# Thresholded attention with a two-layer block on one core: the value product and its scaling placed later in each period, and a score bank for one second-layer group

## The chip, the cores and the metric

The kernel runs on one core of one Trainium2 chip. The metric is the device time of one execution in microseconds (us); the time of a kernel is the median of several executions. A profiled execution has two numbers: its own time, and the span from the first to the last instruction in its trace, which is a little shorter.

## The reference

For 8 batches, 8 heads, 576 positions and a head width of 64, attention with a threshold is followed by two dense layers over 4608 tokens.

```python
scores = (1 / sqrt(64)) * q @ k^T
thresh = max(scores, axis=-1) - tau                    # tau = 0.02
scores = where(scores >= thresh, scores, -1e9)
attn = exp(scores - max(scores));  attn /= sum(attn) + 1e-9
x = (attn @ v), heads side by side                     # 4608 x 512
h = x @ w_in                                           # 512 -> 2048
out = maximum(0.01 * h, h) @ w_out                     # 2048 -> 512
```

## The kernel before

**Periods.** The work is cut into N = 72 periods, and the loop at L653 writes out the instructions of one period after another; no planner reorders them, so each engine works through its own queue in that order. A period has 128 query rows of one batch and four heads (two pairs `c`, two halves `h`), that is four score tiles of 128 x 576. Every second batch also has two "tail" periods for the last 64 rows of each head. Two neighbouring periods give the four heads pairs of 128 tokens, which make one group for the two dense layers.

**Lags.** In the iteration n of the loop three periods are at work: `st`, period n, gets its scores; `before`, period n-1, has its weights `w` turned by DMA transposes on SP's queue (`turn_w`, L391); `due`, period n-2, gets its value product (`pv`, L434, 20 matmuls; 40 for a tail) and is then scaled by the reciprocal sums `by` into `x` (`evacuate`, L453, or L445 for tails, one VectorE instruction).

**TensorE's order in a period before the change.** Scores (`sc`, L297), transposes of the next queries and keys (`tp`, L186), a spread of the reciprocals (L414), then two half periods. The first half has two calls of `layer2` (8 matmuls into `o`, L507), one unit of `layer1` (32 matmuls into `hp`, L474), and `pv(due)`; the second half has again two calls of `layer2` and one of `layer1`. A group has four units of `layer1` (u = 0 to 3) and eight calls of `layer2` (r = 0 to 7). The units stand in the list `l1q`, which `evacuate` fills at the end of a group; a half that finds the list empty has no `layer1`. Each `layer1` releases the second-layer calls of the unit before it into `l2q`. Since two periods give four units and take four, the lists never hold much.

**VectorE's order.** Four copies of the scores out of PSUM with the row minimum (`copy_min`, L338; a copy of turned keys or queries, L249, comes after the first), the reciprocals (L385), the thresholds `th` (L356), then `x` (L453), then three masks (`weights`, L378), which read `th` as their scalar. ScalarE does the exponentials `e` (L367), the fourth tile's weights (L372, L373), the activation `g` of the first layer (L477) and the copy `osb` of a finished `o` (L511), among copies.

**PSUM.** The scores have five banks of their own (`sc`). The tag "h" has two banks, taken in turn by the transposes, `hp`, `pv` and `hp`. The tag "o" has one bank, so the first second-layer call of a group waits for the `osb` copy of the group before. In the last two periods `pv` goes into score banks, and the last group's second layer too (`layer2_last`). After n = 71 there are no scores; what remains of the value products and layers runs out over six more iterations of the loop, the drain.

Of the kernel before, what the change touches and what calls it, by code (L numbers as in the profile page):

```python
# [9 lines left out]
FP32 = mybir.dt.float32  # L10
# [23 lines left out]
def kernel(  # L34
# [341 lines left out]
    def weights(st, n):  # L376
        c, h = t = TILES[n]
        st.last = nc.vector.scalar_tensor_tensor(out=w_of(st, t), in0=st.s[t][:, :], scalar=st.th[:, n : n + 1],  # L378
                                                 in1=st.e[t][:, :], op0=AX.is_le, op1=AX.mult,
                                                 accum_out=st.sum[:, c, h : h + 1])  # L380
# [41 lines left out]
    def pv(st):  # L422
        if st.n >= N - 2:

            st.pv = sc[:, ds(1024 * (N - st.n), 256)].rearrange("d (c q) -> d c q", c=2)
        else:
            st.pv = ps.tile([128, 2, 128], FP32, tag="h", bufs=2, name="pv")
        n = 64 if st.tail else 128
        for c, u in ((c, u) for c in range(2) for u in range(128 // n)):
            pair = 2 * c + u if st.tail else 2 * st.pp + c  # L430
            for i in range(5):
                for h in range(2):
                    blk = i if h == 0 else 9 - i
                    nc.tensor.matmul(out=st.pv[ds(64 * h, 64), c, ts(u, n)], lhsT=v16[st.b % 2][:, pair, blk, :],  # L434
                                     rhs=st.wt[:, c, blk - (blk > 4), ts(u, n)],
                                     start=(i == 0), stop=(i == 4), skip_group_check=True)
# [3 lines left out]
    def evacuate(st):  # L440
        if st.tail:
            if st.b % 2 == 0:
                xs["t"] = sb.tile([128, NP, 128], FP16, tag="xt", bufs=2, name="xt")
            x = xs["t"]
            nc.vector.tensor_tensor(out=x[:, :, ds(64 * (st.b % 2), 64)],  # L445
                                    in0=st.pv[:, :, :].rearrange("d c (u q) -> d (c u) q", u=2),
                                    in1=st.by[:, :, :].rearrange("d c (u q) -> d (c u) q", u=2), op=AX.mult)
            new = [Group(x[:, :, :], (st.b - 1, None))] if st.b % 2 == 1 else []
        else:
            if st.pp == 0:  # L450
                xs["m"] = sb.tile([128, NP, 128], FP16, tag="x", bufs=4, name="x")
            x = xs["m"]
            nc.vector.tensor_tensor(out=x[:, ds(2 * st.pp, 2), :], in0=st.pv[:, :, :], in1=st.by[:, :, :], op=AX.mult)  # L453
            new = [Group(x[:, :, :], (st.b, st.m))] if st.pp == 1 else []
        l1q.extend((g, u) for g in new for u in range(4))
# [43 lines left out]
    def layer2():  # L499
        g, r = l2q.pop(0)  # L500
        if g.where == (B - 1, 3):
            return layer2_last(g, r)
        if r == 0:
            g.o = ps.tile([128, 512], FP32, tag="o", bufs=1, name="o")
        for j in (2 * r, 2 * r + 1):
            for c in range(2):
                nc.tensor.matmul(out=g.o[ds(64 * c, 64), :], lhsT=g.g[:, j, ds(64 * c, 64)],  # L507
                                 rhs=w_out16[:, j, :], start=(j == 0), stop=(j == 15), skip_group_check=True)
        if r == 7:
            g.out = sb.tile([128, 512], FP32, tag="osb", bufs=3, name="osb")  # L510
            nc.scalar.activation(out=g.out[:, :], in_=g.o[:, :], func=AF.Copy, bias=0.0, scale=1.0)  # L511
            stores.append(g)
# [139 lines left out]
    n = 0  # L652
    while n < N + PV_LAG or l1q or pending or l2q or stores:  # L653
        st = periods[n] if n < N else None
        before = periods[n - 1] if 1 <= n <= N else None
        due = periods[n - PV_LAG] if PV_LAG <= n < N + PV_LAG else None
        here = before and before.n < 3
        rest = due and due.n < 3
        plain = 2 if n < 2 or n == 4 else 3
        keys, now32, late = turns_at.get(n, []), early32.get(n, []), late32.get(n)  # L660


        if n == 0:
            def between():
                copy_min(st, 0)
                copy_min(st, 1)
                take_low(k32[1])
                for x in now32:
                    turn32(x)
            scores(st, between)  # L670
            turn32(late)
        elif st:
            scores(st)
        if rest:
            o = ps.tile([128, 1024], FP16, tag="o", bufs=1, name="wp")
            turn_w_here(due, 12, 6, o[:, 0:768])
        bank = turn(keys) if keys else None
        for x in now32 if n else []:
            turn32(x)
        if here:  # L680
            before.wt = sb.tile([128, 2, 9, 128], FP16, tag="wT", bufs=4, name="wT")
            bank = ps.tile([128, 1024], FP16, tag="h", bufs=2, name="tp")
        if due:
            bank = spread(due, bank)
        if here:
            turn_w_here(before, 0, 6, bank[:, 0:768])
        for key in keys:
            take(key, 0, on_act)
        if due:
            take_spread(due, bank)  # L690
        for x in now32:
            take_high(x)
        if here:
            take_w(before, 0, 6, bank[:, 0:768], on_act)
        if st:
            def taken():
                for key in keys:
                    take(key, 1, on_dve)
                if rest:
                    take_w(due, 12, 6, o[:, 0:768], on_dve)  # L700
            copies(st, before, taken, now32)
            exp_plain(st, 0)
            if n == 0:
                exp_plain(st, 1)
                take_high(late)
                take_low(late)
        elif before:
            recip(before)
        work = [lambda key=key: split_pool(key) for key in split_at_.get(n, [])] + pool_at.get(n, [])
        for i, f in enumerate(work):  # L710
            mm = f()
            if i == 0 and before:
                behind_masks(mm, before)
        for key in keys:
            if key[1:] == ("t", "k"):
                widen_keys(key[0])
        if n >= 5:

            for f in small_at.get(n, []):
                f(small=nc.gpsimd)  # L720
        if n < 4:
            idle((4, 10, 8, 4)[n], spare("o"))
        if here:
            o = ps.tile([128, 1024], FP16, tag="o", bufs=1, name="wp")
            if n < 3:
                turn_w_here(before, 6, 6, o[:, 0:768])
        elif before:
            turn_w(before, 1 if st else 2)
        for f in loads_at.get(n, []) + (small_at.get(n, []) if n < 5 else []):
            f()  # L730
        while stores and (n >= N or n not in loads_at or len(stores) > 1):
            store()

        if due and n == 3:
            pv(due)
        if n == 3:
            turn32(late)
            turn_w_here(before, 6, 6, o[:, 0:768])
        for half in range(2):
            if half == 1 and n in (3, 4):  # L740
                exp_steep(st, plain)
            for _ in range(2):
                if l2q:
                    layer2()
            if l1q:
                layer1()
            elif n >= N:
                settle()
            if half == 0:
                if st:  # L750
                    for i in range(1, plain if n else 0):
                        exp_plain(st, i)
                        if n == 3 and i == 1:
                            take_high(late)
                if here:
                    take_w(before, 6, 6, o[:, 0:768], on_act)
                if late and n not in (0, 3):
                    turn32(late)
                    take_high(late)
                if due:  # L760
                    if n != 3:
                        pv(due)
                    evacuate(due)
            elif st and n != 3:
                for i in range(plain + (n == 4), 4):
                    exp_steep(st, i)
        if n == 4:
            take_low(late)
        for i in range(plain if st else 0):
            weights(st, i)  # L770
            if late and n != 4 and n and i == 0:
                take_low(late)
        n += 1
# [33 lines left out]
```

## Time and profile before

| | |
|---|---|
| median of 3 executions | 480.15 us (477.99, 481.57, 480.15) |
| the profiled execution's own time | 480.22 us |
| its span | 478.40 us |
| mean granted TensorE clock | 0.996 |
| TensorE matmuls, busy | 462.8 us, 97% of the span |
| VectorE, busy | 431.6 us, 90% |
| ScalarE, busy | 419.1 us, 88% |
| GpSimd, busy | 216.2 us, 45% |

The busy time of TensorE comes from matmuls whose ends are modelled and overlap, so the pace is better read from the starts of successive blocks in the timeline. In the text below n is the number of the period; scores of period 9 start at 72.69 us, those of period 34 at 226.95 us, those of period 71, the last, at 452.88 us.

### The profile page before, as it was taken

How to read it: one execution, taken by the hardware profiler on the slowest of the kernel's cores; microseconds unless marked ns; L12 is line 12 of the kernel's file. 1: busy time of each engine (PE TensorE's matmuls, PEld its weight loads, DVE VectorE, ACT ScalarE, POOL GpSimd, SP SyncE). 2: the span in 40 equal slices, each digit the busy share in tenths (PEclk: the TensorE clock that was granted, in tenths of full speed). 3: DMA queues.
4: the chain of work that ended last, by engine and by line, in shares of the span. 5: the costliest groups of instructions: out<-in, count | busy, mean ns of one | idle time of the engine just before them, and what ended most of it. 6: DMA issues, size and time to landing. Idle time of an engine off the chain costs nothing.

```text
span 478.4 us, 25135 instructions
## 1 busy us (share of the span) xinstructions
PE 462.8 (97%) x10806; PEld 377.2 (79%) x10806; DVE 431.6 (90%) x1307; ACT 419.1 (88%) x782; POOL 216.2 (45%) x355
## 2 busy tenths in 40 slices
PE   6889889999999999999999999999999999999997
PEld 4667768888888888888888888888888888877776
DVE  3999969999999999999999999999999999999950
ACT  4898968999999999999999998999999999988862
POOL 2645646554465474455465574545357474000000
PEclk9999989999999999999999999999999999999999
DMA  9999998698899968799889987779889996765561
GB/s 174 236 218 195 188 225 164 156 204 178 201 162 192 246 147 210 117 188 203 186 185 182 210 187 176 150 181 202 189 190 173 200 214 129 117 131 124 123 146 46
DMA packets 208767, 84.26 MB, mean 176 GB/s; under 512 B 177648, under 2 KB 203504, under 8 KB 208656
## 3 DMA queue, kind: packets, MB, share of 16 engines
q1 hardware_dynamic: 201616, 75.25, 79.6%
q0 software_dynamic: 5568, 6.95, 7.7%
q8 instruction: 84, 1.38, 1.2%
q10 hardware_dynamic: 1472, 0.46, 0.4%
q14 instruction: 27, 0.22, 0.2%
HBM read 36.70 MB, written 9.44 MB: 96 GB/s over the span
## 4 chain that ended last, share of the span: by engine, by line
PE 87%; DVE 5%; DMA 4%; ACT 2%; issue 1%; SPq 0%; DVEq 0%; ACTq 0%
PE hp L474 25%; PE o L507 24%; PE sc L297 22%; PE pv L434 8%; DMA wT<-w 3%; PE tp L414 3%; PE tp L186 3%; DVE s L338 3%; DMA raw<-in_k_dram 1%; DVE w L378 1%; PE sc L486 1%; ACT g L477 0%; ACT s L372 0%; SPq L86 0%; ACT e L367 0%
## 5 line engine op out<-in xcount | busy, mean ns | idle before, releaser
L338 DVE TENSOR_SCALAR_CACHE_REDUCE s<-sc 128x576 f32<-128x576 f32 x288 | 205.5, 753 | 18.0 <-PE sc L297 17.9
L474 PEld LDWEIGHTS <-win 128*64 128x64 f16 x4608 | 147.1, 110 | 28.8 <-issue 1.3
L378 DVE SCALAR_TENSOR_TENSOR w<-s,th,e 128x576 f16<-128x576 f32 x213 | 163.6, 815 | 0.2
L367 ACT ACTIVATE e<-s,mn 128x576 f16<-128x576 f32 x213 | 157.8, 778 | 0.0
L507 PE MATMUL o<-wout,g 128*64 128x512 f16 x1120 | 145.0, 380 | 0.6 <-ACT osb L511 0.6
L474 PE MATMUL hp<-x,win 128*64 128x128 f16 x4096 | 137.1, 220 | 0.6 <-DVE x L453 0.3
L477 ACT ACTIVATE g<-hp 128x512 f16<-128x512 f32 x144 | 86.1, 598 | 42.8 <-PE hp L474 42.8
L297 PE MATMUL sc<-kT,qT 64*128 64x384 f16 (+7 forms) x1920 | 120.5, 284 | 2.2 <-DVE s L338 1.3
L297 PEld LDWEIGHTS <-qT 64*128 64x128 f16 (+1 forms) x1920 | 90.7, 97 | 18.6 <-issue 2.2
L160 POOL TENSOR_SCALAR scaled<-raw 128x512 f32<-128x512 f32 x53 | 32.7, 616 | 142.3 <-DVE w L378 129.5
L507 PEld LDWEIGHTS <-g 128*64 128x64 f16 x1120 | 56.8, 110 | 28.5 <-issue 0.7
L171 POOL TENSOR_TENSOR half<-scaled,half 128x512 f16<-128x512 f32 (+1 forms) x68 | 71.7, 1054 | 5.8
L373 ACT ACTIVATE w<-s,minus_tau 128x576 f16<-128x576 f32 x75 | 58.2, 775 | 2.4
L372 ACT ACTIVATE s<-s,th 128x576 f32<-128x576 f32 x75 | 57.5, 767 | 0.7 <-DVE th L356 0.7
L434 PE MATMUL pv<-wT,v 128*64 128x128 f16 (+1 forms) x1560 | 51.6, 214 | 3.7 <-DMA wT<-w 2.7
L434 PEld LDWEIGHTS <-v 128*64 128x64 f16 x1600 | 45.7, 110 | 5.1 <-DMA wT<-w 2.7
L167 POOL CAST half<-scaled 128x512 f16<-128x512 f32 (+1 forms) x68 | 38.3, 563 | 4.4
L453 DVE TENSOR_TENSOR x<-pv,by 128x256 f16<-128x256 f32 x62 | 26.3, 423 | 4.3 <-PE pv L434 4.2
L420 ACT COPY by<-tp 128x256 f16<-128x256 f16 x71 | 26.4, 372 | 0.0
L186 PEld LDWEIGHTS <-half 64*128 64x128 f16 x968 | 24.3, 95 | 2.6 <-issue 1.7
L186 PE MATMUL tp<-ident,half 64*128 64x64 f16 x968 | 24.2, 190 | 0.4 <-issue 0.4
L113 POOL CAST v<-vraw 128x256 f16<-128x256 f32 x64 | 24.5, 417 | 0.0
(64 smaller groups left out, 338.5 us busy)
## 6 DMA issues: line engine op xcount, KB each, us to landing
vraw<-in_v_dram SPq DMA_DIRECT2D x16, 512.0 KB, 5.5
out_dram<-osb SPq DMA_DIRECT2D x31, 256.0 KB, 3.9
raw<-in_q_dram SPq DMA_DIRECT2D x13, 512.0 KB, 4.8
raw<-in_k_dram SPq DMA_DIRECT2D x13, 512.0 KB, 5.5
win<-in_moe_w_in_dram POOLq DMA_DIRECT2D x4, 512.0 KB, 10.6
wout<-in_moe_w_out_dram POOLq DMA_DIRECT2D x4, 512.0 KB, 12.4
raw<-in_q_dram SPq DMA_DIRECT2D x12, 128.0 KB, 3.8
raw<-in_k_dram SPq DMA_DIRECT2D x10, 128.0 KB, 4.4
```

Source lines behind the costliest of these rows:

```text
L171: nc.gpsimd.tensor_tensor(out=halves[key][:, 1, 0:n, :, :], in0=scaled.pop(key)[:, 0:n, :, :], in1=halves[key][:, 0, 0:n, :, :], op=AX.sub ...
L186: nc.tensor.transpose(tps[key][r][:, x, t, :], half[rows, x, t, :, :].rearrange("p h d -> p (h d)"), ident[rows, rows])
L297: yield nc.tensor.matmul(out=o, lhsT=lhs, rhs=turned[st.b, "k"][rows, kx, pair, ds(key0, n)], start=(i == 0), stop=(i == 2), skip_group_ch ...
L338: return nc.vector.tensor_scalar(out=st.s[TILES[n]][:, :], in0=sc[:, ds(PLACE[TILES[n]], 576)], scalar1=-1.0 / UNIT, scalar2=None, op0=AX. ...
L367: nc.scalar.activation(out=st.e[t][:, :], in_=st.s[t][:, :], func=AF.Exp, bias=st.mn[:, n : n + 1], scale=-1.0)
L372: nc.scalar.activation(out=z, in_=z, func=AF.Prelu, bias=st.th[:, n : n + 1], scale=-1.0, alpha=1e20)
L373: nc.scalar.activation(out=w_of(st, t), in_=z, func=AF.Exp, bias=minus_tau[:, :], scale=1.0, accum_out=st.sum[:, c, h : h + 1])
L378: st.last = nc.vector.scalar_tensor_tensor(out=w_of(st, t), in0=st.s[t][:, :], scalar=st.th[:, n : n + 1], in1=st.e[t][:, :], op0=AX.is_le ...
L434: nc.tensor.matmul(out=st.pv[ds(64 * h, 64), c, ts(u, n)], lhsT=v16[st.b % 2][:, pair, blk, :], rhs=st.wt[:, c, blk - (blk > 4), ts(u, n)] ...
L474: nc.tensor.matmul(out=hp[ds(64 * c, 64), jj, :], lhsT=w_in16[:, i, ds(128 * (4 * u + jj) + 64 * c, 64)], rhs=g.x[:, i, :], start=(i == 0) ...
L477: nc.scalar.activation(out=g.g[:, ds(4 * u, 4), :], in_=hp[:, :, :], func=AF.Prelu, bias=0.0, scale=1.0, alpha=0.01)
L507: nc.tensor.matmul(out=g.o[ds(64 * c, 64), :], lhsT=g.g[:, j, ds(64 * c, 64)], rhs=w_out16[:, j, :], start=(j == 0), stop=(j == 15), skip_ ...
```

## The change

From period 9 to period 71 the value product `pv(due)` is issued in the second half, behind its two `layer2` calls and ahead of its `layer1`, and no longer at the end of the first half. The scaling `evacuate(due)` is issued among the masks, behind the second of three. Because `evacuate` also fills `l1q`, units become available half a period later in program order. The group of batch 7, m = 2, the last but one, gets columns 512 to 1023 of the scores for its `o`, and no longer the bank of the tag "o". In the drain (n of 72 and above) `pv` and `evacuate` stay where they were.

```diff
         if r == 0:
-            g.o = ps.tile([128, 512], FP32, tag="o", bufs=1, name="o")
+            g.o = sc[:, 512:1024] if g.where == (B - 1, 2) else ps.tile([128, 512], FP32, tag="o", bufs=1, name="o")
...
             for _ in range(2):
                 if l2q:
                     layer2()
+            if half == 1 and 9 <= n < N:
+
+                pv(due)
             if l1q:
                 layer1()
...
-                if due:
+                if due and not 9 <= n < N:
                     if n != 3:
                         pv(due)
                     evacuate(due)
...
         for i in range(plain if st else 0):
             weights(st, i)
+            if i == 1 and 9 <= n < N:
+                evacuate(due)
             if late and n != 4 and n and i == 0:
                 take_low(late)
```

## The prediction

> **What bounds the kernel now.** I read the chain of waits first, then the busy times by stretch, then one ordinary period on TensorE and VectorE, and last the two places where the change has an end: periods 9 to 11 and the drain. The chain is 87% TensorE, and from the scores of period 9 to the end of those of period 71 TensorE has no idle time to speak of:
>
> ```profile
> 72.70:458.80 386.10, 385.75 (x9305) 315.35 (x9304) 370.65 (x1135) 354.45 (x660) 180.82 (x288) 1.00 0.87 175
> ```
>
> The columns after the stretch are its length and the busy times of TensorE's matmuls and weight loads, VectorE, ScalarE and GpSimd, then the granted clock, the DMA share and GB/s. An ordinary period, n = 34, from the timeline (start, length, engine, line):
>
> ```profile
> 226.95 1.64 PE L297 MATMUL sc<-kT,qT 64*128 64x384 f16 x24
> 228.43 0.40 PE L186 MATMUL tp<-ident,half 64*128 64x64 f16 x16
> 228.76 0.30 PE L414 MATMUL tp<-ident,rec 128*64 128x128 f16 x4
> 228.89 1.03 PE L507 MATMUL o<-wout,g 128*64 128x512 f16 x8
> 229.76 1.06 PE L474 MATMUL hp<-x,win 128*64 128x128 f16 x32
> 230.65 0.72 PE L434 MATMUL pv<-wT,v 128*64 128x128 f16 x20
> 231.21 1.03 PE L507 MATMUL o<-wout,g 128*64 128x512 f16 x8
> 232.07 1.06 PE L474 MATMUL hp<-x,win 128*64 128x128 f16 x32
> ```
>
> From start to start: scores 1.48, transposes 0.33, spread 0.13, second layer 0.87, first layer 0.89, pv 0.56, second layer 0.86, first layer 0.99, and the next scores begin at 233.06: 6.11 us without a hole. VectorE in the same period:
>
> ```profile
> 231.48 0.17 DVE L356 TENSOR_SCALAR th<-mn 128x4 f32<-128x4 f32 x1
> 231.56 0.42 DVE L453 TENSOR_TENSOR x<-pv,by 128x256 f16<-128x256 f32 x1
> 231.90 0.81 DVE L378 SCALAR_TENSOR_TENSOR w<-s,th,e 128x576 f16<-128x576 f32 x1
> ...
> 234.43 0.76 DVE L338 TENSOR_SCALAR_CACHE_REDUCE s<-sc 128x576 f32<-128x576 f32 x1 [0.23 <-PE sc L297]
> ```
>
> VectorE waits only 0.23 us per period, for the scores. TensorE sets the pace, with VectorE close behind. So a wait that is moved can only pay where TensorE really stands still.
>
> **The change, part by part.** The sum is made against the profiled execution, 480.22 us (span 478.40 and 1.82 around it), which is 0.07 above the median shown.
>
> *Waits of pv for its turned weights.* In most periods the step from hp of the first half to pv takes 0.89. In periods 21, 43, 51 and 61 it takes 1.13, 1.34, 1.01 and 0.99, because the transpose (L391 on SP's queue, 3.2 to 9.5 us from issue to landing) is late. The sum of the excess is 0.24 + 0.45 + 0.12 + 0.10 = 0.91. After the change the second-layer block, 0.86, stands ahead of pv and covers each of these. Term: -0.91. If the cover did not help it would be 0. The large pv wait of 2.42 us at 59 us is in period 7 and stays.
>
> *The move on TensorE itself.* Same 20 matmuls, same shapes, the neighbours change from hp, pv, second layer, hp to hp, second layer, pv, hp. Hp before second layer takes 0.90 in the drain, second layer before hp 0.86, pv before second layer 0.55 to 0.58. pv before hp is not shown; by these rows it costs between 0.01 less and 0.03 more, over 63 periods -0.6 to +1.9. I take 0, the blocks being alike in tile form. Banks: pv and hp come in the same order in the tag "h", so no bank changes its neighbour. The next period's transposes need pv's bank back, so they now wait for x; x ends near 233.5 (below), they start at 234.54. First-layer units now use x in the next period, at 235.87 and no longer at 232.07. The osb copy moves with r = 7 into the second half, behind the exponentials; ScalarE waits 0.39 and 0.22 us for hp in such a period, and the next group's first call comes 2 us after it. SP's stores keep their place behind the transposes. All of this costs nothing as long as these margins stand.
>
> *VectorE.* x moves behind the second mask. pv ends near 232.2 and x would start at 233.2, so x does not wait. But the first mask now stands right behind th, which it reads. Now x starts 0.08 after th starts, and hides th's way out. The nearest row for the new pair is period 1:
>
> ```profile
> 19.34 0.44 DVE L356 TENSOR_SCALAR th<-mn 128x4 f32<-128x4 f32 x1
> 19.88 0.93 DVE L378 SCALAR_TENSOR_TENSOR w<-s,th,e 128x576 f16<-128x576 f32 x1
> ```
>
> The mask starts 0.10 after th's end. With th at its usual 0.17 that is 0.27 from start to start, against 0.08: 0.19 more per period, inside the 0.23 that VectorE waits. Behind the waiting mask stand the other masks, x and the next copies, and L249 of the next period, for whose bank the next hp waits; its margin in period 34 to 35 is 235.87 - 235.53 = 0.34. Where th takes 0.28 (periods 18, 36, 54) the cost is 0.30 against 0.23, and in the two-key periods 13, 31, 49 the wait is only 0.17: 3 x 0.07 + 3 x 0.02, term +0.3. Bounds: 0 per period, and 0.54 - 0.08 = 0.46 if th always took what it took in period 1. The Trainium skill, "VectorE: DVE Perf Modes", section on the DRAIN you can't avoid, has it that a Vector instruction waits for the one before to empty the pipe anyway, and that a semaphore between two costs nothing extra. By it the term is 0 and the sum 0.3 lower. The rows of x and th, which overlap by 0.09, do not agree.
>
> *The skipped units.* In period 9 x comes too late for the second half, which finds `l1q` empty: no hp (0.89). So the first half of period 10 finds no second-layer call (0.86). All later units are half a period behind, and the drain gets these 1.75 us. What TensorE gains in periods 9 and 10 depends on VectorE, which has no wait at the start of period 10. It works at L249 there until 81.47:
>
> ```profile
> 81.05 0.42 DVE L249 COPY kT<-tp 128x512 f16<-128x512 f16 x1
> ```
>
> The hp of period 10, now at 81.90, uses the bank that L249 reads; with 0.15 more on VectorE in period 9 it can start at about 81.68, so 0.22 earlier, and not 1.75. By period 12 VectorE's waits have absorbed the rest, and the 0.22 stays. TensorE stands still for 1.53 us in period 10. Term: +1.53; bounds 0 (all of it gained) and 1.75.
>
> *The drain.* Before, the first call of group (7, 2) waits for the copy of group (7, 1):
>
> ```profile
> 461.19 0.60 ACT L511 ACTIVATE osb<-o 128x512 f32<-128x512 f32 x1
> ...
> 461.83 1.05 PE L507 MATMUL o<-wout,g 128*64 128x512 f16 x8 [0.58 <-ACT osb L511]
> ```
>
> From pv at 460.53 to this block are 1.30 instead of 0.56, so 0.74. With the score bank, and with a second-layer pair and an hp between r = 7 and the next r = 0, the wait is gone; either would do. Next late is the last pv: it comes 0.74 earlier, at 464.7, and its second transpose was issued at 461.6, 3.2 us at least from landing. Term: -0.74 + 0.19 = -0.55, between -0.74 and 0.
>
> Sum: -0.91 + 0 + 0.3 + 1.53 - 0.55 = +0.37, so 480.22 + 0.37 = 480.6 us.
>
> **The rivals.** *The deferred unit is free* (TensorE runs ahead in periods 9 and 10 and keeps all of it): 480.22 - 0.91 - 0.74 = 478.6. For it: in all other places VectorE has 0.23 per period to catch up. Against it: the bank that L249 reads.
>
> *The clock falls in period 10.* In the trace a standstill of 2.42 us is followed by a stretch at half clock:
>
> ```profile
> 28.40:31.80 3.40, 2.38 (x50) 1.87 (x45) 3.40 (x12) 3.40 (x7) 2.39 (x3) 1.00 1.23 198
> 59.30:62.70 3.40, 1.20 (x26) 0.93 (x28) 0.37 (x2) 1.64 (x3) 0.48 (x1) 0.99 1.27 188
> 62.70:66.10 3.40, 3.40 (x45) 2.64 (x43) 2.90 (x8) 0.92 (x2) 0.00 (x0) 0.50 1.15 255
> ```
>
> TensorE's busy time is the number behind the length: 1.20 of 3.40 us brought the clock to 0.50, 2.38 did not. Period 10 would have 1.9 of 3.4, between them. The price from the rows: second layer 1.14 for 0.86, hp 1.85 for 1.02, scores 1.95 for 1.56, together 1.5. Then 480.6 + 1.5 = 482.1. The Trainium skill, "TensorE: Matmul & The Clock Gate", Part 1, wants at least one idle window of about 3.4 us before the clock halves; by it the 1.5 us would not do, and this rival would have no chance. The trace has it fall after 2.42, so the rule does not hold here as stated.
>
> *VectorE becomes the bound.* Place: the first mask behind th. Price: what the hand-over takes above the 0.23 of each period. At a th of 0.20 (the mean of L356 is 198 ns) it is 0.22 and decides nothing; with th at 0.28 it is 0.30, 62 x 0.07 = 4.3, so 484.9; at 0.46 it is 62 x 0.23 = 14 and 494.9. I put this rival at 486. For it: VectorE has little to spare, and th is slow wherever GpSimd works beside it. Against it: th takes 0.17 in nearly every period from 12 on.
>
> **How the numbers follow.** Two medians of this kernel can be told apart by about 1%, 4.8 us. The forecast has 0.62, the free unit 0.12, the clock 0.11, VectorE's bound 0.15. The first three lie within 1%. Of the last most is slower by over 1%: 0.13. Faster by over 1% would need 4.8 us, and TensorE's waits from period 9 on are 0.91 and 0.74 together; I leave 0.03 for what the trace of one execution does not show. The remaining 0.84 is within 1%. The range: below, the free unit at 478.6 less 0.8 for the spread of the executions (lowest 477.99); above, the forecast with 1.9 for pv before hp, and the clock, and into VectorE's bound: 485.3.
>
> **What would show it right or wrong.** Right: pv never waits for a transpose from period 9 on; blocks of an ordinary period still add up to 6.11; VectorE's wait for the scores falls from 0.23 to some 0.05; one hole of about 1.5 us on TensorE in period 10 behind the spread, released by L249; no wait for osb in the drain; the last scores of period 71 start about 0.8 us earlier than 452.88 (0.22 + 0.91 - 0.3), and the drain is 1.2 longer. Wrong: no wait left at VectorE's first copy and ordinary periods of more than 6.15 us (VectorE's bound); clock rows of 0.50 near 82 us; a period shorter than 6.11, which would mean that TensorE had hidden waits that I do not see.

## The result, and the profile after

The change takes 482.30 us (median of 9 executions, 481.21 to 483.64) against 480.15 us for the kernel before. The ratio is 1.0045, interval 1.0026 to 1.0064: slower by a little less than half a per cent, and within the 1% that the forecast called no change. A second measurement gave 1.0054 (1.0028 to 1.0079).

The profiled execution of the change took 482.30, with a span of 480.50. The two spans divide as follows, by the start of the scores (`sc`, L297) of a period.

| stretch | before | change | forecast | measured |
|---|---|---|---|---|
| up to the scores of period 9 | 72.69 | 71.51 | 0 | -1.18 |
| periods 9 and 10 | 12.51 | 12.50 | -0.22 | -0.01 |
| periods 11 to 70 | 367.68 | 367.53 | -0.61 | -0.15 |
| scores of period 71 to the end | 25.52 | 28.96 | +1.20 | +3.44 |
| span | 478.40 | 480.50 | +0.37 | +2.10 |

The first row is code that the change leaves alone. The profile of before has 3.4 us at half clock there, behind its wait in period 7; the change's profile has a granted clock of 1.00 all through. From one kernel's profile to the next in this study the scores of period 9 start anywhere from 69.5 to 73.9 us, so the reading below starts there. The scores of period 9 themselves took 1.56 in the profile of before and 1.77 to 1.79 in each of the 13 other profiles of this study, with the old order or the new. So 12.51 is low: four more profiles with the old order there (the bank alone, the moves from 64 and from 40, and before with two added instructions, all below) have 12.72 or 12.73. Against those the change gained 0.22 or 0.23 in periods 9 and 10.

An ordinary period of the change, n = 34, on TensorE and then on VectorE (timeline: start, length, engine, line):

```profile
226.00 1.65 PE L297 MATMUL sc<-kT,qT 64*128 64x384 f16 x24
...
228.81 1.06 PE L474 MATMUL hp<-x,win 128*64 128x128 f16 x32
229.70 1.03 PE L507 MATMUL o<-wout,g 128*64 128x512 f16 x8
230.56 0.72 PE L434 MATMUL pv<-wT,v 128*64 128x128 f16 x20
231.12 1.06 PE L474 MATMUL hp<-x,win 128*64 128x128 f16 x32
232.11 0.33 PE L297 MATMUL sc<-kT,qT 64*128 64x384 f16 x2
```

```profile
230.53 0.17 DVE L356 TENSOR_SCALAR th<-mn 128x4 f32<-128x4 f32 x1
230.79 0.82 DVE L378 SCALAR_TENSOR_TENSOR w<-s,th,e 128x576 f16<-128x576 f32 x1
231.53 0.81 DVE L378 SCALAR_TENSOR_TENSOR w<-s,th,e 128x576 f16<-128x576 f32 x1
232.27 0.42 DVE L453 TENSOR_TENSOR x<-pv,by 128x256 f16<-128x256 f32 x1
232.61 0.81 DVE L378 SCALAR_TENSOR_TENSOR w<-s,th,e 128x576 f16<-128x576 f32 x1
233.48 0.76 DVE L338 TENSOR_SCALAR_CACHE_REDUCE s<-sc 128x576 f32<-128x576 f32 x1
```

The period still takes 6.11 (226.00 to 232.11), and pv ahead of hp costs 0.56 like pv ahead of the second layer. On VectorE the first mask starts 0.26 behind th, where x started 0.08 behind it. The wait of 0.23 at the first copy of the next scores is no longer marked; about 0.06 is left there: behind the last mask stands the read of its accumulator (not shown), which ends at 233.42, and the copy starts at 233.48.

Period 10 has the hole, behind VectorE's copy L249:

```profile
80.21 0.41 DVE L249 COPY kT<-tp 128x512 f16<-128x512 f16 x1
...
80.68 1.08 PE L474 MATMUL hp<-x,win 128*64 128x128 f16 x32 [1.13 <-DVE kT L249]
```

From the spread, at 79.25, to this hp are 1.43 instead of 0.13, so the hole is 1.30. The transposes ahead of the spread took 0.57 instead of 0.34, which makes 1.53 together.

The drain, on TensorE:

```profile
456.43 1.06 PE L474 MATMUL hp<-x,win 128*64 128x128 f16 x32
457.95 0.30 PE L414 MATMUL tp<-ident,rec 128*64 128x128 f16 x4 [0.47 <-DVE x L453]
...
462.13 0.30 PE L414 MATMUL sc<-ident,rec 128*64 128x128 f16 x4
463.27 1.05 PE L507 MATMUL sc<-wout,g 128*64 128x512 f16 x8 [0.84 <-ACT by L420]
...
465.03 0.75 PE L434 MATMUL sc<-wT,v 128*64 128x128 f16 x20
466.37 1.05 PE L507 MATMUL sc<-wout,g 128*64 128x512 f16 x8 [0.59 <-DVE x L453]
```

The wait for osb is gone, but three others are there. Against the usual steps (0.90 for hp, 0.11 for a spread, 0.56 for pv) they cost 456.43 to 457.95 less 0.90 = 0.62, 462.13 to 463.27 less 0.11 = 1.03, and 465.03 to 466.37 less 0.56 = 0.78. The second and third stand ahead of the second layer of group (7, 2) in its score bank, and their releasers, the copy `by` (in columns 0 to 511) and the last x (columns 1024 to 1279), work on other columns of the scores than `o` (512 to 1023).

### The profile page after: what moved, and what is told of

Its sections match the earlier page's. It is cut to its first block, busy times and chain, and to the rows that moved or that the text cites. A ratio compares the mean times of both kernels' runs of the same rounds, so it can differ in the third digit from the quotient of the medians.

```text
span 480.5 us, 25071 instructions
## 1 busy us (share of the span) xinstructions
PE 463.4 (96%) x10806; PEld 376.2 (78%) x10806; DVE 437.7 (91%) x1307; ACT 419.9 (87%) x782; POOL 217.9 (45%) x355
## 4 chain that ended last, share of the span: by engine, by line
PE 83%; DVE 10%; ACT 3%; issue 2%; DMA 2%; POOL 0%; DVEq 0%; POOLq 0%; ACTq 0%
PE hp L474 24%; PE o L507 22%; PE sc L297 20%; PE pv L434 7%; DVE s L338 5%; DVE w L378 3%; PE tp L414 3%; PE tp L186 3%; DMA wT<-w 2%; PE sc L507 1%; PE sc L543 1%; ACT e L367 1%; PE sc L486 1%; ACT g L477 1%; DVE x L453 0%
## 5 line engine op out<-in xcount | busy, mean ns | idle before, releaser
L338 DVE TENSOR_SCALAR_CACHE_REDUCE s<-sc 128x576 f32<-128x576 f32 x288 | 205.4, 752 | 5.1 <-PE sc L297 3.0
L378 DVE SCALAR_TENSOR_TENSOR w<-s,th,e 128x576 f16<-128x576 f32 x213 | 170.1, 824 | 6.2 <-DVE th L356 0.4
L474 PEld LDWEIGHTS <-win 128*64 128x64 f16 x4608 | 142.3, 110 | 17.7 <-issue 2.1
L507 PE MATMUL o<-wout,g 128*64 128x512 f16 x1088 | 140.3, 379 | 0.0
L297 PE MATMUL sc<-kT,qT 64*128 64x384 f16 (+7 forms) x1920 | 120.7, 284 | 2.6 <-DVE s L338 1.3
L297 PEld LDWEIGHTS <-qT 64*128 64x128 f16 (+1 forms) x1920 | 90.3, 97 | 19.5 <-issue 2.4
L171 POOL TENSOR_TENSOR half<-scaled,half 128x512 f16<-128x512 f32 (+1 forms) x68 | 71.7, 1055 | 5.8
L434 PEld LDWEIGHTS <-v 128*64 128x64 f16 x1600 | 49.4, 110 | 17.3 <-issue 3.1
```

The source lines that it names most:

```text
L171: nc.gpsimd.tensor_tensor(out=halves[key][:, 1, 0:n, :, :], in0=scaled.pop(key)[:, 0:n, :, :], in1=halves[key][:, 0, 0:n, :, :], op=AX.sub ...
L297: yield nc.tensor.matmul(out=o, lhsT=lhs, rhs=turned[st.b, "k"][rows, kx, pair, ds(key0, n)], start=(i == 0), stop=(i == 2), skip_group_ch ...
L338: return nc.vector.tensor_scalar(out=st.s[TILES[n]][:, :], in0=sc[:, ds(PLACE[TILES[n]], 576)], scalar1=-1.0 / UNIT, scalar2=None, op0=AX. ...
L474: nc.tensor.matmul(out=hp[ds(64 * c, 64), jj, :], lhsT=w_in16[:, i, ds(128 * (4 * u + jj) + 64 * c, 64)], rhs=g.x[:, i, :], start=(i == 0) ...
```

## The experiments

### The two parts, apart, and the bank without its waits

Theory: the score bank itself makes two of the drain's waits, because the schedule orders operations by the whole tile `sc` and not by its columns; the move makes the third and the longer drain. Rival: the waits come from the later x, whatever bank holds `o`.

The move alone puts `o` of group (7, 2) back under the tag:

```diff
-            g.o = sc[:, 512:1024] if g.where == (B - 1, 2) else ps.tile([128, 512], FP32, tag="o", bufs=1, name="o")
+            g.o = ps.tile([128, 512], FP32, tag="o", bufs=1, name="o")
```

> The value product and x moved as in the change, but the second layer of group (7, 2) stays in the bank of the tag o. In the trace of the change two second-layer blocks of that group wait in the drain for operations that use other columns of the scores: 1.03 us more than usual ahead of the first (released by the copy of the reciprocals, by) and 0.78 ahead of the second (released by x). Theory (the score bank made these waits): both go, no wait for osb comes in their place, since the copy of the group before ends 0.2 us ahead of the first block: 1.8 us less than the change, 480.5. The drain from the scores of period 71 to the end of the span then takes 27.1 instead of 28.96. Rival (the waits belong to the later x and by themselves): the drain stays near 28.9 and the time near 482.3.

The bank alone makes the reverse edit of that line on the kernel before.

> Only the score bank for group (7, 2), on the kernel before. Theory (the bank makes waits): the 0.74 us wait for osb goes, but its place is taken by a wait for x of period 70, and the next two blocks wait for by and for the last x, about 0.8 and 0.6: some 1.4 above before, 481.5. Rival (the bank only removes the wait for osb): 479.4.

In the other two, each matmul of that group's second layer (`mm`) is told that it does not depend on `by` of the last period and on x of the last two, which are kept in the list `others`. The lines that say so:

```diff
...
+                if g.where == (B - 1, 2):
+                    for y in others:
+                        tc.declare_no_dep(mm.ins, y.ins, reason="other banks")
```

> The whole change, with the second layer of group (7, 2) told that by and x of the last two periods use other banks. Theory: as with the move alone, 480.5, the waits for by and x gone. Rival (banks really collide, or the last value product is late anyway): the drain keeps more than 1 us of waits and the time stays over 481.5.

> The score bank on the kernel before, with the same statement that by and x use other banks. Theory (the drain of before loses 0.74 us to the wait for osb and nothing is late behind it but, by 0.2, the last transpose): 0.5 to 0.7 below before, 479.5. Rival (the last transpose or x takes up all of it): same as before, 480.1.

| kernel | scores of 71 to the end | median us | ratio to before (interval) |
|---|---|---|---|
| before | 25.52 | 480.15; 481.23 beside these four | |
| change | 28.96 | 482.30 | 1.0045 (1.0026 to 1.0064) |
| move alone | 27.18 | 480.38 | 0.9977 (0.9954 to 0.9999) |
| bank alone | 27.38 | 482.78 | 1.0030 (1.0001 to 1.0059) |
| change, free bank | 27.19 | 481.04 | 1.0008 (0.9980 to 1.0037) |
| before, free bank | 24.82 | 481.65 | 1.0013 (0.9984 to 1.0043) |

The drains decide it. The move alone takes 1.78 off the change's drain, 1.8 was expected, and it has no wait for osb: the move removes that wait without the bank. The free bank does the same as the move alone with `o` in the scores, so the banks do not collide and the waits were made by the order alone. The bank alone costs 1.86 on the kernel before, where 1.4 was expected, and the waits in its drain (who waited for whom: us in total, times, the longest) are the expected ones:

```profile
PE sc L507 <- DVE x L453: 1.2, 2, 0.6
PE sc L507 <- ACT by L420: 0.8, 1, 0.8
```

Made free, it saves 0.70 of 25.52, as expected for the osb wait. The time as a whole cannot show so small a gain: the interval of before with the free bank is 0.6% wide and lies about 1.

### The hole behind the skipped units

Theory: TensorE cannot run ahead of VectorE while each period's first hp waits for the bank that VectorE's L249 reads. The move alone, started at period 64 (no more transposes of keys and queries) and at period 40. Only the condition is changed, here for 64, and likewise in its two other places:

```diff
-            if half == 1 and 9 <= n < N:
+            if half == 1 and 64 <= n < N:
```

> The move alone (bank of the tag o kept), but from period 64 on, where no keys and queries are turned any more and L249 is absent. In the change the units left out in periods 9 and 10 (1.75 us of TensorE's work) bought nothing: the two periods together take 12.50, as before (12.51). Theory (the hp of period 10 waits for the bank that VectorE's L249 reads, so TensorE can't run ahead of VectorE): without L249 most of the 1.75 is kept; periods 64 and 65 together take about 10.2 instead of 11.80. Rival (VectorE's work as such, or the banks of the scores, holds TensorE whatever L249 does): 11.5 or more.

> The same move from period 40 on, where keys and queries are still turned in every period. Theory (L249 again): periods 40 and 41 together take 12.0 to 12.2, as before (12.10), with one hole of 1 to 1.5 us in TensorE in period 41, released by VectorE's L249 or x. Rival (the place at 9 is special, because VectorE had no wait left there): at least 0.5 us of the 1.75 is gained, 11.6 or less.

Both expectations named the wrong periods: from these starts the list of units runs empty one period later, in 65 and 66, and in 41 and 42. Both runs are single executions, 479.64 from 64 and 484.64 from 40; in the second, late transposes cost 4.6 in periods 21 to 43. Read in the right periods, the first shows this: periods 65 and 66 take 10.17 where before takes 11.85, so 1.68 of the 1.75 is gained at first; 0.35 is given back in period 67, where the spread waits for x, and the start itself costs 0.28. From the scores of 64 to those of 71 the gain is 1.06 (40.29 against 41.35). From 64 on VectorE has less work in all, so this run by itself does not tell the bank from VectorE's load; the marks at the holes, which name L249, speak for the bank.

From 40, periods 41 and 42 take 11.83 instead of 12.23, a gain of 0.40, and the hole is in 42:

```profile
279.76 0.42 DVE L249 COPY qT<-tp 128x512 f16<-128x512 f16 x1
...
280.24 0.97 PE L474 MATMUL hp<-x,win 128*64 128x128 f16 x28 [1.12 <-DVE qT L249]
```

Period 40 loses 0.46, of which 0.42 is a wait for osb, because in the first period of the new order pv no longer stands between the two groups. So periods 40 to 42 together keep nothing (18.28 against 18.22). The mechanism holds: with L249 a marked wait of 1.1, without it most of the units' time is kept. The rival asked for a gain of at least 0.5; 0.40 falls short of it, and at 9, read against the four profiles named above, 0.22 or 0.23 were gained. So the place makes some difference, but a small one.

### VectorE's margin and the place of x

> The value product moved as in the change, x at its old place in VectorE's queue, ahead of the three masks (bank of the tag o kept). Theory (VectorE has 0.23 us per period and would wait for pv, which ends some 0.6 later than x could start): some 0.4 us more per period over 62 periods, about 25 us, 505. Rival (TensorE bounds the kernel and x's place is free): 480 to 482.

Against the move alone:

```diff
+        if 9 <= n < N:
+            evacuate(due)
         for i in range(plain if st else 0):
             weights(st, i)
-            if i == 1 and 9 <= n < N:
-                evacuate(due)
```

It took 490.92 (one execution; span 489.10), and periods of 6.11 became 6.32. On VectorE, x now waits for pv and there is no wait left at the next scores (L338):

```profile
230.37 0.42 DVE L453 TENSOR_TENSOR x<-pv,by 128x256 f16<-128x256 f32 x1 [0.43 <-PE pv L434]
...
232.93 0.75 DVE L338 TENSOR_SCALAR_CACHE_REDUCE s<-sc 128x576 f32<-128x576 f32 x1
```

The theory's direction holds and its size was double: 0.43 is the wait and the 0.23 comes off it, which leaves 0.2 per period. The estimate had the wait at 0.6. So x between the masks is worth about 10 us once pv is late.

The next two add VectorE work, to before and to the move alone (`pads` is a tile for the unused result):

```diff
...
+        if st.n >= 12:
+            for i in range(2):
+                nc.vector.tensor_copy(out=pads[:, ts(i, 4)], in_=minus_tau[:, :].to_broadcast([128, 4]))
         if before:
             recip(before)
```

> The kernel before with two more VectorE instructions on 128x4 elements in every period from 12 on, ahead of the reciprocals, 0.12 us each from start to start; their result is not used. Theory (VectorE waits 0.23 us per period, and a little more work there costs nothing): periods of 6.11 stay within 0.03, the time within 1.5 us of before. Rival (VectorE already sets the pace somewhere in the period): 0.1 to 0.24 more per period, 6 to 14 us.

> The same two instructions in the move alone (bank of the tag o kept). Theory (the hand-over from th to the first mask has used up all but some 0.05 of VectorE's margin): ordinary periods rise from 6.11 to about 6.30, some 10 us more than the move alone, 491. Rival (VectorE still has its margin): 6.11 to 6.14, 480 to 482.

Before with the two instructions took 478.99 (one execution). In its period 34, where before shows 0.23, VectorE's wait is still 0.16:

```profile
233.50 0.76 DVE L339 TENSOR_SCALAR_CACHE_REDUCE s<-sc 128x576 f32<-128x576 f32 x1 [0.16 <-PE sc L298]
```

The two take 0.14 from start to start, but the way from the reciprocals to x shrinks from 0.20 to 0.14. So the dose was 0.07 and not 0.24. Periods 9 to 70 took 380.19, as before, but that is a balance: this execution has none of the 0.98 that before lost to late transposes (see below) and 0.22 more in period 9, while periods 19, 37 and 55 are 0.17 to 0.19 longer and 13, 31 and 49 by 0.07. The other periods stay within 0.03, as the theory said; in these six, which lost 0.75 together, the old order has no room for even this dose.

In the move alone it cost more: 485.76 (one execution), and periods 9 to 70 rose from 379.53 to 383.42. Period 34 and its neighbours stayed at 6.11; 25 others rose by 0.1 to 0.3, and why these did the runs do not show. So VectorE's margin is smaller in the new order than in the old, but the expected 10 us were wrong by the dose.

The last one asks what the long periods 13 and 49 of the change (6.60 and 6.49 instead of 6.31) come from.

> The move alone, with the reciprocals issued behind the thresholds th and no longer ahead of them, so that th's way out is covered by another instruction (0.12 us from start to start). Theory (the hand-over from th to the first mask eats 0.18 of VectorE's 0.23 us, and the long periods 13, 19, 31, 49 and 55 come from it): th to first mask stays near 0.26, VectorE's copies start to wait for scores again by some 0.1, and periods 13 and 49 lose 0.1 to 0.2 each. Rival (those periods are long because GpSimd slows the masks there): they stay at 6.6 and 6.5.

Against the move alone:

```diff
-        if before:
-            recip(before)
         nc.vector.tensor_scalar(out=st.th[:, :], in0=st.mn[:, :], scalar1=1.0, scalar2=tau_f, op0=AX.mult, op1=AX.add)
+        if before:
+            recip(before)
```

It took 480.44 (one execution), and periods 13 and 49 stayed at 6.59 and 6.48. The rival's figures came out for these two. In period 12 of this kernel:

```profile
94.19 0.41 DVE L354 TENSOR_SCALAR th<-mn 128x4 f32<-128x4 f32 x1
...
94.66 0.67 POOL L171 TENSOR_TENSOR half<-scaled,half 128x256 f16<-128x256 f32 x1
...
94.69 1.25 DVE L378 SCALAR_TENSOR_TENSOR w<-s,th,e 128x576 f16<-128x576 f32 x1
```

Here the first mask takes 1.25 and not 0.81; GpSimd's subtraction (L171) runs beside it from 94.66 to 95.33. The same instructions in the kernel before:

```profile
95.97 0.17 DVE L356 TENSOR_SCALAR th<-mn 128x4 f32<-128x4 f32 x1
96.05 0.67 POOL L171 TENSOR_TENSOR half<-scaled,half 128x256 f16<-128x256 f32 x1
...
96.40 0.94 DVE L378 SCALAR_TENSOR_TENSOR w<-s,th,e 128x576 f16<-128x576 f32 x1
```

There x stands between th and the mask, so the mask overlaps the subtraction for 0.32 instead of 0.64 and takes 0.94. The mask is not all of it: th itself takes 0.41 instead of 0.17, in the change too (and 0.31 in period 48), and from th to the mask are then 0.50 instead of 0.26. So the hand-over may have a part in periods 13 and 49, and this run cannot clear it: the swap took nothing from it. In period 34 th now starts 0.12 behind the start of the accumulator read that ends the last copy, while in the move alone the reciprocals started together with that read; from its start to the first mask are 0.38 here and 0.37 there.

### The end of the move, and the change again

> The move from period 9 to period 70, with period 71 in the old order, and the bank of the tag o kept. Theory (in period 72 the spread waits for the bank of pv and so for x of period 71, 0.62 us in the move alone; with pv and x of period 71 at their old places it does not): the drain takes 26.5 from the scores of period 71 instead of 27.2, the time is 0.6 below the move alone, 479.8 where that was 480.4. Rival (a later wait takes it back, the last transposes above all): 27.2, as the move alone.

The line for `o` is that of the move alone; the condition changes here and likewise in its two other places:

```diff
-            if half == 1 and 9 <= n < N:
+            if half == 1 and 9 <= n < N - 1:
```

The rival is right: the drain takes 27.29. The wait for x in period 72 is gone, and the last pv waits instead for the second of the last two transposes, so that from pv to the second layer are 1.19 instead of 0.56:

```profile
465.10 0.47 PE L434 MATMUL sc<-wT,v 128*64 128x128 f16 x10
466.01 0.47 PE L434 MATMUL sc<-wT,v 128*64 128x128 f16 x10 [0.44 <-DMA wT<-w]
466.29 1.06 PE L507 MATMUL o<-wout,g 128*64 128x512 f16 x8
```

> The change once more, on the same chip as the others. Theory (the score bank costs 1.8 and the late x of period 71 0.6): 2.4 us above the move until period 70, 482.2, and the stretch from the scores of period 9 to those of period 71 the same in both within the waits for transposes. Rival (the two differ by the state of the chip): no difference.

Medians of 12 executions each on one chip: the change 482.57, 1.0054 (1.0028 to 1.0079) of before, the move until period 70 481.48, 1.0012 (0.9989 to 1.0035). The drains differ by 28.96 - 27.29 = 1.67 and the medians by 1.1. The stretch from 9 to 71 was not the same in the two profiles: 379.42 and 382.26. Nearly all of the difference of 2.84 is in periods 37, 48, 49 and 51, at places inside score, first-layer and value blocks that the trace marks as waiting for nothing it shows, so nothing follows from it for the move.

No version beats both kernels beyond doubt. The move alone is the lowest in ratio, with an interval that ends at 0.9999.

## Why the prediction was right, and where it was off

The forecast of no change within 1%, at 480.6 and a range of 477.8 to 485.3, holds: 482.3 is a loss of 0.45%. Luck has a part in that. The 1% is 4.8 us wide and covers one step that failed: from the scores of period 9 on, the profile lost 3.28 where the sum had +0.37, and the two spans differ by less only because 1.18 of it is made up at the start, which the change does not touch. By the terms of the sum:

**The drain: -0.55 forecast, +1.69 measured** (3.44 less the 1.75 of work that moved there). This is the term that failed. The step, in the prediction's words, was "with the score bank, and with a second-layer pair and an hp between r = 7 and the next r = 0, the wait is gone; either would do". The 0.74 did go, and it goes with the move alone, so either would do; but the bank was costed at nothing, and it makes waits of 1.03 and 0.78, shown by the four kernels that take the bank and its order apart. The third wait, 0.62, is the late x of period 71. The margin of about a microsecond between x and the next use of pv's bank was read from a period with scores ahead; in period 72 there are none. Moving the end of the move by one period removes this wait and lets the last transposes take its place. In the change itself the 0.19 for the last transpose, which the prediction's rows (issue at 461.6, 3.2 to landing) do not give, was not seen: pv at 465.03 follows its hp by the usual 0.90.

**The skipped units: +1.53 forecast, +1.74 measured against the profile of before, +1.52 or +1.53 against the four other profiles with the old order at this place.** Mechanism and place were right: a hole in period 10, released by L249, then hp at 80.68. Relative to the scores of period 9 that is 9.17. The profile of before has 9.21, so only 0.04 gained and not 0.22; but its scores of period 9 are the short ones, and the four others have 9.41 to 9.43, so about 0.25. So the forecast was right to a few hundredths, and it is the profile of before that stands apart.

**Waits of pv for transposes: -0.91 forecast.** Periods 21, 43, 51 and 61 gave back 0.98 (differences of the four periods). The size is one execution's: counted in the same way over periods 11 to 63, it is 0.91 in the profile of before, 2.1 with the bank alone, 2.9 with the free bank on before, 2.4 in the kernel that moves from 64 on, and 0 with the two added VectorE instructions. The eight profiles with the move from period 9 on show no such wait up to period 70. But the second-layer block ahead of pv does not cover every late transpose. The kernel that moves from 40 on waits in the new order too, in period 43:

```profile
289.84 0.75 PE L434 MATMUL pv<-wT,v 128*64 128x128 f16 x20 [1.51 <-DMA wT<-w]
```

So the term is likely but not shown as a gain of the move: no kernel took the transposes' lateness away by itself, and it differs as much between executions of one order.

**VectorE: +0.3 forecast, +0.5 to +1.1 measured.** The hand-over from th to the first mask was 0.26 in an ordinary period against a forecast of 0.27, and VectorE's 0.23 went almost wholly, as said. Periods 13, 31 and 49 cost 0.29, 0.06 and 0.18, not for the reason given (0.02 each, a short margin): the mask ahead of each meets GpSimd's subtraction (1.26 each time), and ahead of 13 and 49 th takes 0.41 and 0.31. That th keeps to 0.17 "in nearly every period from 12 on" was read from the old order. There, from 12 on, it was above 0.2 in periods 18, 36 and 54 alone; in the change it is above 0.2 in 13 periods, all of them others. Nor is th slow wherever GpSimd works: it took 0.17 beside the subtraction in the rows of before shown above. Periods 18, 36 and 54, where 0.07 each was expected, cost nothing; th took 0.17 there. Periods 19 and 55 lost 0.24 and 0.32 in the change's profile, 0.11 and nothing in that of the move alone; their cause stays open. The Trainium skill, "VectorE: DVE Perf Modes", section "The DRAIN you can't avoid", has a semaphore between two Vector instructions cost nothing extra, measured on a chain of tensor copies. For the small th it does cost: the mask that reads th starts 0.18 later behind it than x did, 0.26 less 0.08. The same section says that an instruction that is not held starts earlier, so the overlap of x and th need not speak against it, as the prediction had it.

**TensorE's own blocks: 0 forecast, and -0.2 measured.** pv ahead of hp takes 0.56. Five periods that took 6.16 or 6.28 before (18, 28, 36, 46, 54) are 0.04 to 0.05 shorter.

Of the rivals, the free unit did not happen, except where L249 is absent. The clock did not fall: the profile after shows a granted clock of 1.00 around the hole, with TensorE busy 2.27 of 3.40 us (the first number behind the length; the clock is third from the end). So the 1.9 of 3.4 that this rival assumed was not reached, and what the clock does between 1.20 and 2.27 stays open.

```profile
79.30:82.70 3.40, 2.27 (x56) 1.86 (x56) 3.40 (x13) 2.44 (x5) 2.79 (x5) 1.00 0.61 123
82.70:86.10 3.40, 3.40 (x120) 3.00 (x116) 3.31 (x10) 3.37 (x7) 1.78 (x4) 1.00 0.50 107
```

VectorE did not become the bound, but came within 0.06 us per period of it, and the kernel with x ahead of the masks shows what lies behind that line: 0.21 per period.

## What to carry to other kernels

An order that fills one engine leaves no room to defer work for nothing: units that are skipped once to shift a schedule come back whole at the end (1.75 us here), and they are gained at the start only if the other engines can run ahead too. Before a part of a large tile is lent to something else, ask which instructions are ordered behind the whole tile, and look for them in the last, thinly filled stretch, where the margins read from an ordinary period do not hold. And read a wait that depends on transfers from several executions: here it was 0 in one execution of the old order, 0.9 in another and 2.9 in a third. The same goes for the ends of a change: the short scores of period 9 in a single profile hid a gain that four others show.

## What the runs showed of the hardware that was not expected

A mask of 128 x 576 on VectorE takes 0.81. Beside some of GpSimd's instructions it takes longer: 0.94 where it overlapped the subtraction of 0.67 for 0.32, and 1.26 where it overlapped it for 0.64, so moving it by 0.3 us changed its length. Other masks beside GpSimd stayed at 0.81. The mask that reads th starts 0.09 behind th's end, whether th takes 0.17 or 0.41, while x, which does not read it, starts 0.08 behind th's start in an ordinary period of the old order. Two further instructions of 128 x 4 elements ahead of the reciprocals cost VectorE only 0.07 together. The transposes through DMA took 3.2 to 9.5 us from issue to landing in the profile of before, and up to 14.5 in that of the change with the free bank.
